# Seven block products for eight in the projections of the last two attention units, and a written order of issue

## Chip, cores and metric

The kernel runs on one core of one Trainium2 chip. The metric is the time of one execution on the device in microseconds (us); the time of a version is the median over its runs.

## The reference

A layer of two branches over the same input `x` (1 x 2048 x 640), mixed by a gate, all in float32.

```python
qkv = (x @ wqkv).reshape(B, S, 3, H, Dh)          # H = 32 heads of 20
idx = pos[:, None] - arange(8) * 2                 # eight keys, two apart
attn = softmax(where(idx >= 0, q . k[idx], -1e9) * scale)
a = (attn @ v[idx]).reshape(B, S, 640) @ wo
h = x @ w1 + b1                                    # 640 -> 1728
b = (h * tanh(softplus(h))) @ w2                   # Mish, 1728 -> 640
g = sigmoid((x * gate_w).sum(-1))
out = g * a + (1 - g) * b
```

## The kernel before

**Matrix work.** Each float32 operand is held as a rounded high part and the rest, a "pair" tile of 2 x 512 columns; one 128-deep product is three matmuls (`mm3`, lines 932 to 934: high by high, high by rest, rest by high). ACT makes the high part (line 873), DVE or POOL subtracts it from the operand for the rest (line 876). Operands come by DMA into `raw`, `z` or `hb` tiles, or into the pair's second half itself.

**Attention.** The work is cut into eight units `u = 4 * P + hq`: `P` is a half of the sequence (two blocks `tb` of 512 rows), `hq` a quarter of the heads. `qkv(u, half)` projects 512 rows in four PSUM banks: each bank is 128 rows by 496 columns (160 of q, 320 of k and v, 16 left-over columns of `w1`) over five blocks `kc` of 128, so 15 matmuls in a run. ACT empties a bank in three pieces (lines 1080 to 1084). DVE then does the unit's attention in sixteen instructions of 2560 columns (lines 985, 988, 1023, 1032) and small ones between them.

**First dense layer.** `quad(q, P, R)` (listed as T) makes two blocks of hidden columns for two row blocks by seven products of blocks for eight: sums of `x` blocks (`XS`, made once in each half by `sums_of_x`), sums of weight blocks, copies of one bank into another on ACT (line 1374) so that matmuls go on from a partial sum, and one addition of a kept product on DVE (line 1407). The projections of all eight units are plain before the change.

**Then** the second dense layer (`mlp2`, 7 products, `sums_of_w2` for its weights, listed as S), and the output projection. `FRONT` lists the first part's pieces in order, `BACK` says at which step of `mlp2` further pieces are put in.

**What sets the order.** All instructions are recorded as tasks, and `Plan.run` issues them. Before, it steps through a model of the five engines and takes, whenever an engine is free, the most urgent task that is ready; five tables of numbers by task (`MOVED`, `HELD_BACK`, `NEEDED`, `RANKED`, `ENGINE`) shift each task's place, delay, urgency, rank or engine. Tasks of kind "ANY" (rests, sums) go to DVE or POOL. On the chip each engine runs its list in this order and waits on semaphores; SP issues nearly all DMAs, POOL those that add in memory.

## Time and profile before

| | |
|---|---|
| median of 3 runs | 617.6 us (616.7 to 618.37) |
| profiled execution, its own time | 616.73 us |
| span in its profile | 615.0 us |
| PE busy | 608.9 us, 2693 matmuls |
| DVE, ACT, POOL busy | 577.1, 387.9, 311.2 us |

Busy times are unions of an engine's instructions. Matmuls overlap in the pipeline, so their rate is read from the distance of their starts.

### The profile page before, as it was taken

How to read it: one execution, taken by the hardware profiler on the slowest of the kernel's cores; microseconds unless marked ns; L12 is line 12 of the kernel's file. 1: busy time of each engine (PE TensorE's matmuls, PEld its weight loads, DVE VectorE, ACT ScalarE, POOL GpSimd, SP SyncE). 2: the span in 40 equal slices, each digit the busy share in tenths (PEclk: the TensorE clock that was granted, in tenths of full speed). 3: DMA queues.
4: the chain of work that ended last, by engine and by line, in shares of the span. 5: the costliest groups of instructions: out<-in, count | busy, mean ns of one | idle time of the engine just before them, and what ended most of it. 6: DMA issues, size and time to landing. Idle time of an engine off the chain costs nothing.

```text
span 615.0 us, 8940 instructions
## 1 busy us (share of the span) xinstructions
PE 608.9 (99%) x2693; PEld 504.7 (82%) x2693; DVE 577.1 (94%) x531; ACT 387.9 (63%) x854; POOL 311.2 (51%) x293
## 2 busy tenths in 40 slices
PE   8999999999999999999999999999999999999997
PEld 6888888888888888788888888888888888888885
DVE  4999999999998999999999999999999999999962
ACT  5746774768575767876666654583867574684721
POOL 2736566476283654654457657668554444601200
PEclk9999999999999999999999999999999999999999
DMA  8864679999999689999998999789999998996423
GB/s 301 254 192 149 178 220 305 280 252 305 257 268 300 172 240 273 261 242 259 291 267 219 286 289 290 243 245 299 332 377 352 283 386 276 321 354 197 147 89 119
DMA packets 106128, 159.43 MB, mean 259 GB/s; under 512 B 12112, under 2 KB 47952, under 8 KB 106048
## 3 DMA queue, kind: packets, MB, share of 16 engines
q1 hardware_dynamic: 98976, 146.01, 73.2%
q0 software_dynamic: 7104, 12.85, 13.7%
q8 instruction: 21, 0.34, 0.2%
q14 instruction: 27, 0.22, 0.1%
HBM read 91.90 MB, written 64.36 MB: 254 GB/s over the span
## 4 chain that ended last, share of the span: by engine, by line
PE 98%; DMA 1%; ACT 0%; SPq 0%; issue 0%; ACTq 0%
PE bank L932 32%; PE bank L934 32%; PE bank L933 32%; DMA z<-in_wq 1%; PE bank L1687 1%; PE bank L1688 1%; PE bank L1074 0%; SPq L882 0%; ACT pair L873 0%; ACT kvq L1801 0%; ACT kvq L1080 0%; ACT kvq L1082 0%; ACT hx L1084 0%; ACT zt L1086 0%; ACTq L1801 0%
## 5 line engine op out<-in xcount | busy, mean ns | idle before, releaser
L932 PE MATMUL bank<-pair,pair 128*128 128x512 f32 (+2 forms) x774 | 299.5, 387 | 0.4 <-ACT zt L1086 0.4
L933 PE MATMUL bank<-pair,pair 128*128 128x512 f32 (+2 forms) x774 | 299.7, 387 | 0.0
L934 PE MATMUL bank<-pair,pair 128*128 128x512 f32 (+2 forms) x774 | 299.7, 387 | 0.0
L932 PEld LDWEIGHTS bank<-pair,pair 128*128 128x128 f32 x774 | 145.4, 188 | 29.4 <-ACT zt L1086 0.8
L934 PEld LDWEIGHTS bank<-pair,pair 128*128 128x128 f32 x774 | 145.4, 188 | 28.7
L933 PEld LDWEIGHTS bank<-pair,pair 128*128 128x128 f32 x774 | 145.3, 188 | 28.7
L876 POOL TENSOR_TENSOR pair<-raw,pair 128x512 fp32r<-128x512 f32 (+3 forms) x82 | 104.8, 1303 | 86.9 <-ACT pair L873 30.2
L876 POOL TENSOR_TENSOR pair<-pair 128x512 fp32r<-128x512 f32 (+1 forms) x65 | 82.9, 1294 | 56.5 <-ACT pair L873 21.6
L873 ACT ACTIVATE pair<-pair 128x512 fp32r<-128x512 f32 (+1 forms) x139 | 79.6, 612 | 38.8 <-DMA pair<-act 18.7
L1023 DVE TENSOR_TENSOR pr<-kvq,side 128x2560 f32<-128x2560 f32 x32 | 90.3, 2822 | 1.1
L1032 DVE TENSOR_REDUCE kvq<-pr 128x320 f32<-128x2560 f32 x32 | 90.1, 2816 | 0.6
L988 DVE TENSOR_REDUCE lg<-pr 128x128 f32<-128x2560 f32 x32 | 90.0, 2812 | 0.6
L985 DVE TENSOR_TENSOR pr<-kvq,side 128x2560 f32<-128x2560 f32 x32 | 89.8, 2806 | 0.6 <-ACT lg L1000 0.5
L873 ACT ACTIVATE pair<-raw 128x512 fp32r<-128x512 f32 (+3 forms) x125 | 72.6, 613 | 18.5 <-PE bank L934 5.2
L1080 ACT ACTIVATE kvq<-bank 128x320 f32<-128x320 f32 x64 | 27.7, 434 | 49.1 <-PE bank L934 48.9
L876 DVE TENSOR_TENSOR pair<-pair 128x512 fp32r<-128x512 f32 (+1 forms) x74 | 46.7, 671 | 0.9 <-ACT pair L873 0.9
L932 PE MATMUL bank<-kvq,pair 128*128 128x512 f32 x102 | 40.0, 392 | 0.0
L933 PE MATMUL bank<-kvq,pair 128*128 128x512 f32 x102 | 39.8, 390 | 0.0
L934 PE MATMUL bank<-kvq,pair 128*128 128x512 f32 x102 | 39.8, 390 | 0.0
L1227 POOL TENSOR_TENSOR raw<-raw,raw 128x256 f32<-128x256 f32 (+1 forms) x25 | 24.4, 978 | 22.6 <-DVE side L1026 7.8
L876 DVE TENSOR_TENSOR pair<-raw,pair 128x512 fp32r<-128x512 f32 (+3 forms) x43 | 32.9, 785 | 1.7 <-ACT pair L873 1.7
L1374 ACT ACTIVATE bank<-bank 128x512 f32<-128x512 f32 x36 | 21.0, 584 | 13.7 <-PE bank L934 13.5
(119 smaller groups left out, 590.9 us busy)
## 6 DMA issues: line engine op xcount, KB each, us to landing
pair<-actt SPq DMA_DIRECT2D x54, 256.0 KB, 5.0
pair<-act SPq DMA_DIRECT2D x38, 256.0 KB, 4.8
raw<-in_w SPq DMA_DIRECT2D x34, 256.0 KB, 4.7
raw<-in_wq SPq DMA_DIRECT2D x30, 248.0 KB, 4.5
raw<-in_x SPq DMA_DIRECT2D x29, 256.0 KB, 5.1
actt<-hb SPq DMA_DIRECT2D x28, 256.0 KB, 3.6
actt<-z SPq DMA_DIRECT2D x24, 256.0 KB, 6.6
act<-z SPq DMA_DIRECT2D x24, 256.0 KB, 5.7
```

Of the source, the lines that this page charges most:

```text
L873: a = add("ACT", act_ns(n), lambda: A.activation(hi(), raw(), AF.Copy), after, rank=rank, take=take, hold=hold, kind="hi")
L876: return (V if e == "DVE" else G).tensor_tensor(lo(), raw(), hi().bitcast(F32), op=OP.subtract)
L932: nc.tensor.matmul(ps, ah, bh, start=first, stop=False, skip_group_check=more)
L933: nc.tensor.matmul(ps, ah, bl, start=False, stop=False, skip_group_check=more)
L934: nc.tensor.matmul(ps, al, bh, start=False, stop=last, skip_group_check=more)
L985: return V.tensor_tensor(pr, window(kv, s0, 0), qs[:, :, None, :].to_broadcast([128, 2, W, QF]), op=OP.mult)
L988: return V.tensor_reduce(lg_w[:, s0:s0 + 2], pr.rearrange("p s w (h d) -> p s w h d", d=DH), op=OP.add, axis=AX.X)
L1023: return V.tensor_tensor(twos, vw, pw[:, :, :, :, None, None].to_broadcast([128, 2, W, HQ, DH // 2, 2]), op=OP.mult)
L1032: return step("DVE", 2820, lambda: V.tensor_reduce(q[:, s0:s0 + 2].rearrange("p s (f j) -> p f s j", j=2), by_place, op=OP.add, axis=AX.X) ...
L1080: a = add("ACT", 330, lambda: A.activation(kv[:, 7 + s], ps.t[:, QF:3 * QF].rearrange("p (a b) -> p a b", a=2), AF.Copy), [done] + before, ...
L1227: return (V if e == "DVE" else G).tensor_tensor(t.t[:, i:i + n], a.t[:, j:j + n], b.t[:, k:k + n], op=op)
L1374: return add("ACT", 590, lambda: A.activation(to.t, of.t, AF.Copy), after, rank=-0.6, take=[to], hold=[of], kind=kind)
```

## The change

Units 6 and 7 (the second half of the sequence, head quarters 2 and 3) are no longer projected by `qkv` but together by a new function `qkv_two` (listed as D). The 2 x 2 blocks are rows `tb` 2 and 3 by even and odd `kc` of `x` (the sums `XS` are those of the quads), and even and odd `kc` by head quarter of the weights; the fifth `kc` is added plainly. `sums_of_wq(kp)` (U) makes four sums of weight blocks, stores them to memory, and `qkv_two` loads them again. What followed the projections in `qkv` (the halo copies, the attention) is now in `placed_unit`. S4 and S1, the sums of `w2` for two of its seven blocks, move from FRONT into BACK.

`Plan.run` no longer chooses: `ISSUE` lists each engine's tasks by number, `TAKEN` says on which engine the buffer of each ring is taken next, and the run places buffers only. The five tables are gone. A POOL task of kind "ANY" is made to follow the DVE instruction beside which the list puts it.

```diff
 FRONT = """q1 s0 Q00 Q01 w0 r00 Q10 q2 F0 F1 r10 Q11 r20 T00 r40 T10 Q20 S0 T20 r30 Q21 q3 T30 T40 Q30 w1
-r50 y3 q4 T50 Q31 x2 s1 F2 r01 Q40 F3 M0 T01 r11 r21 q5 r31 r51 S3 M1 T11 Q41 T21 Q50 r41 T31
-q6 Q51 T41 S2 q7 Q60 T51 H Q61 Q70 Q71 S4 S1"""
-BACK = "23O0 13V0 0M2 7S6 21O1 2S5 35G 0M3 21V1"
+r50 y3 q4 T50 Q31 x2 s1 F2 r01 Q40 F3 M0 T01 r11 r21 q5 r31 r51 S3 M1 T11 Q41 T21 Q50 U0 r41 T31
+U1 Q51 T41 S2 T51 D"""
+BACK = "23O0 13V0 1S4 0M2 7S6 3S1 21O1 5S5 35G 0M3 21V1"
...
+ENGINES = ("PE", "ACT", "DVE", "POOL", "SP")
+ISSUE = {
+    "PE": """1 96-110 115 120 125 130 135 140 145 290 232 240 236 244 298 294 267 263 302 376 377 380 381 386 388 425 389 390 426 429 430
...
+TAKEN = {
+    "bank": ("0000000000000000000000010101101100101010000000011100111000100101000000000010011010101000010101001010010000010110011"
...
+            if t.eng == "POOL" and t.both:
+                if single:
+                    s = max(s, over["DVE"] - 80)
+                elif before and s < over["DVE"]:
+                    s = max(s, before.own + 100)
+                if ahead and ahead[0] < s + t.ns - 50 and ahead[1].alone:
+                    s = max(s, ahead[0] + ahead[1].ns)
+            if t.eng == "DVE" and t.alone:
+                s = max(s, beside - 50)
...
+            if e == "POOL" and t.both:
+                gate = before if s < over["DVE"] - 80 else last
+                if gate and gate.ins and ins:
+                    self.follow(ins, gate.ins)
...
+    def sums_of_wq(kp):
+        r = {}
+        for hq, kc in ((2, 2 * kp), (3, 2 * kp), (3, 2 * kp + 1), (2, 2 * kp + 1)):
+            r[hq, kc - 2 * kp] = raw = raw_buf()
+            raw.ready = dma(lambda raw=raw: raw.t[:, :NCOL], lambda hq=hq, kc=kc: wq[hq, kc][:, :NCOL], rank=0.6, take=[raw], size=NCOL * 512)
+        b11, b21, b12, b22 = r[2, 0], r[2, 1], r[3, 0], r[3, 1]
+        t1 = sum_into((b11, 0), (b12, 0), (b11, 0), OP.subtract, [b11.ready, b12.ready], NCOL, rank=AHEAD)
+        t3 = sum_into((b12, 0), (b22, 0), (b12, 0), OP.subtract, [t1, b22.ready], NCOL, rank=AHEAD)
+        t2 = sum_into((b22, 0), (b22, 0), (b11, 0), OP.subtract, [t3], NCOL, rank=AHEAD)
+        t4 = sum_into((b21, 0), (b21, 0), (b22, 0), OP.subtract, [t2, b21.ready], NCOL, rank=AHEAD)
+        for i, raw, t in ((1, b11, t1), (3, b12, t3), (2, b22, t2), (4, b21, t4)):
+            wq_sum[kp, i] = [dma(lambda kp=kp, i=i: wq_d[kp, i], lambda raw=raw: raw.t[:, :NCOL], [t], rank=0.7, hold=[raw], size=NCOL * 512)]
+    def qkv_two():
+        n, t0, t1 = NCOL, 2, 3
+        def plain(hq, kc):
+            return load_pair(lambda: wq[hq, kc][:, :n], "ANY", n=n)
+        def summed(i):
+            return [load_pair(lambda kp=kp: wq_d[kp, i], "ANY", n=n, after=wq_sum[kp, i], inner=True) for kp in range(2)]
+        def xs(tb, b):
+            return [X[tb, 2 * kp + b] for kp in range(2)]
+        def s(i):
+            return [XS[kp, i] for kp in range(2)]
+        def phase(banks, xt, wt, after, start, stop, sums=False):
+            ends = []
+            for i, ps in enumerate(banks):
+                def run(i=i, ps=ps):
+                    for k, (a, b) in enumerate(zip(xt, wt)):
+                        mm3(ps.t[:, :n], tuple(a.t[:, j, i * 128:(i + 1) * 128] for j in range(2)), tuple(b.t[:, j, :n] for j in range(2)),
+                            start and k == 0, stop and k == len(xt) - 1, not start)
+                t = pe_add(3 * len(xt) * mm_ns(n), run, after[i] + sum((x.ready for x in xt + wt), []), take=[ps] if start else [], hold=[ps] + xt + wt)
+                ends.append([t])
+                if sums:
+                    s_uses.append(t)
+            return ends
+        def copy(to, of, after, take):
+            return add("ACT", 590, lambda: A.activation(to.t[:, :n], of.t[:, :n], AF.Copy), after, rank=-0.6, take=[to] if take else [], hold=[to, of])
+        def copies(tos, ofs, after, take):
+            return [[copy(to, of, t, take)] for to, of, t in zip(tos, ofs, after)]
+        def plus_five(to, five, after):
+            return add("DVE", 690, lambda: V.tensor_tensor(to.t[:, :n], five.t[:, :n], to.t[:, :n], op=OP.add), after, rank=SOON, hold=[to, five])
+        def both(*lists):
+            return [sum(x, []) for x in zip(*lists)]
+        def out_of(u, banks, half, ends):
+            ev = unit.setdefault(u, {})
+            for i, (ps, t) in enumerate(zip(banks, ends)):
+                ev[4 * half + i] = qkv_evac(u, 1, u - 4, 4 * half + i, ps, t[0])
+        none = [[] for _ in range(4)]
+        one = [ps_buf(n) for _ in range(4)]
+        b11 = [plain(2, 2 * kp) for kp in range(2)]
+        p1 = phase(one, xs(t0, 0), b11, none, True, True)
+        two_ = [ps_buf(0) for _ in range(4)]
+        c1 = copies(two_, one, p1, True)
+        b21 = [plain(2, 2 * kp + 1) for kp in range(2)] + [plain(2, 4)]
+        p2 = phase(one, xs(t0, 1) + [X[t0, 4]], b21, c1, False, True)
+        out_of(6, one, 0, p2)
+        p6 = phase(two_, s(2), summed(2), c1, False, False, True)
+        z = [z_buf() for _ in range(4)]
+        c3 = copies(z, two_, p6, True)
+        p7 = phase(two_, s(3), summed(3), c3, False, False, True)
+        w = [raw_buf(), h_buf(), raw_buf(), h_buf()]
+        c4 = copies(w, two_, p7, True)
+        p4 = phase(two_, xs(t1, 1) + [X[t1, 4]], summed(4) + [b21[2]], c4, False, True)
+        out_of(6, two_, 1, p4)
+        five = [ps_buf(n) for _ in range(4)]
+        p5 = phase(five, s(1), summed(1), none, True, True, True)
+        listed["H"]()
+        z5 = [[plus_five(a, b, t + c)] for a, b, t, c in zip(z, five, p5, c3)]
+        w5 = [[plus_five(a, b, t + c)] for a, b, t, c in zip(w, five, p5, c4)]
+        b22 = [plain(3, 2 * kp + 1) for kp in range(2)] + [plain(3, 4)]
+        three = [ps_buf(0) for _ in range(4)]
+        c5 = copies(three, z, z5, True)
+        p3 = phase(three, s(4) + [X[t0, 4]], b22, c5, False, True)
+        placed_unit(6)
+        out_of(7, three, 0, p3)
+        four = [ps_buf(0) for _ in range(4)]
+        c6 = copies(four, w, w5, True)
+        p8 = phase(four, [X[t1, 4]], [b22[2]], c6, False, True)
+        out_of(7, four, 1, p8)
+        placed_unit(7)
```

`phase` runs three matmuls for each operand pair in each of four banks; `copies` are ACT copies of one bank (or kept tile) to another; `plus_five` is a DVE addition of the fifth product to a kept one.

**First place: PE, in the projections of unit 6.** A name is a tile with its number; of a matmul's operands the weights' pair stands first, the rows' pair second. Before, `bank0_63` gets the last of its 15 matmuls over five blocks, three matmuls of a quad (512 columns) follow, and then the next bank is begun.

```order
L932 MATMUL bank0_63<-pair17_3114,pair0_1802 128x496
L933 MATMUL bank0_63<-pair17_3114,pair0_1802 128x496
L934 MATMUL bank0_63<-pair17_3114,pair0_1802 128x496
L932 MATMUL bank2_65<-pair0_1802,pair6_2843 128x512
L933 MATMUL bank2_65<-pair0_1802,pair6_2843 128x512
L934 MATMUL bank2_65<-pair0_1802,pair6_2843 128x512
L932 MATMUL bank6_69<-pair18_3025,pair10_2031 128x496 [waits DVE_49]
```

After the change (lines 511 to 513 are `mm3`) a bank gets two blocks in its first piece, and another bank, which was begun earlier and has been copied since, goes on.

```order
L511 MATMUL bank0_63<-pair12_3153,pair19_1801 128x496
L512 MATMUL bank0_63<-pair12_3153,pair19_1801 128x496
L513 MATMUL bank0_63<-pair12_3153,pair19_1801 128x496
L511 MATMUL bank6_69<-pair9_3081,pair2_1854 128x496 [waits Activation_49]
L512 MATMUL bank6_69<-pair9_3081,pair2_1854 128x496
L513 MATMUL bank6_69<-pair9_3081,pair2_1854 128x496
L511 MATMUL bank6_69<-pair1_3229,pair3_1936 128x496
L512 MATMUL bank6_69<-pair1_3229,pair3_1936 128x496 [waits Pool_49]
```

The run of 15 is cut into pieces: the second piece of `bank6_69` now waits for ACT, and at its second weight block for POOL, which makes that block's rest.

**Second place: DVE, in the attention of units 4 and 5, while units 6 and 7 are projected.** `pr` and `lg` are products and logits, `sm` the softmax's sums. Before, one rest of a weight block (`pair1_3298`) stands ahead of the softmax's small instructions.

```order
L988 TENSOR_REDUCE lg_223<-pr_225 128x2x8x8 [waits DVE_49]
L876 TENSOR_TENSOR pair1_3298<-raw7_3076,pair1_3298 128x496 [waits Activation_49]
L1015 TENSOR_REDUCE sm_227<-lg_223 128x32 [waits Activation_49]
L1016 RECIPROCAL sm_227<-sm_227 128x32 [waits DVE_49]
L1017 TENSOR_TENSOR sm_227<-sm_227,gate_80 128x32 [waits DVE_49]
L1026 TENSOR_TENSOR side_224<-lg_223,sm_227 128x2x8x8 [waits DVE_49,Activation_49]
L1023 TENSOR_TENSOR pr_225<-kvq1_221,side_224 128x16x80x2 [waits DVE_49]
```

After the change four of the eight `plus_five` (line 776, a PSUM bank added to a kept tile) stand in such a place.

```order
L564 TENSOR_TENSOR pr_225<-kvq1_221,side_224 128x2560 [waits DMAHW3_49]
L567 TENSOR_REDUCE lg_223<-pr_225 128x2x8x8 [waits DVE_49]
L776 TENSOR_TENSOR z2_3419<-bank4_67,z2_3419 128x496 [waits DMAHW0_49,DMAHW7_49,PE_49,Activation_49]
L776 TENSOR_TENSOR z0_3394<-bank2_65,z0_3394 128x496 [waits PE_49,DMAHW4_49,Activation_49,Pool_49]
L776 TENSOR_TENSOR raw1_3457<-bank2_65,raw1_3457 128x496 [waits DMAHW5_49,Activation_49]
L594 TENSOR_REDUCE sm_227<-lg_223 128x32 [waits Activation_49]
L595 RECIPROCAL sm_227<-sm_227 128x32 [waits DVE_49]
L776 TENSOR_TENSOR hb1_3454<-bank4_67,hb1_3454 128x496 [waits DMAHW3_49,DMAHW0_49,DMAHW5_49,DMASW5_49,DMAHW6_49,DMASW1_49,DMASW0_49]
L596 TENSOR_TENSOR sm_227<-sm_227,gate_80 128x32 [waits DVE_49]
L605 TENSOR_TENSOR side_224<-lg_223,sm_227 128x2x8x8 [waits DVE_49]
```

The rest has left DVE here, and additions have come that name PE among their waits, with the softmax's sums and the next product `pr` queued behind them.

**Third place: POOL, while unit 6 is projected.** Lines 876 and 455 make rests; a row with `raw` inside reads a plain operand, one with the pair alone an operand that landed in the pair. Before, the plain weight blocks of units 6 and 7 stand here, and sums of the one quad whose results are added on chip (line 1328).

```order
L876 TENSOR_TENSOR pair2_3038<-raw7_2868,pair2_3038 128x496 [waits DVE_49,DMAHW6_49,PE_49,Activation_49]
L1170 DMA actt2_1_3_151<-actt1_1_3_137 128x512 [waits DMAHW7_49,DMASW5_49,DMASW0_49]
L876 TENSOR_TENSOR pair4_3072<-raw8_2910,pair4_3072 128x496 [waits DVE_49,DMAHW6_49,PE_49,Activation_49]
L876 TENSOR_TENSOR pair7_3084<-raw0_2914,pair7_3084 128x496 [waits Activation_49]
L876 TENSOR_TENSOR pair3_3151<-raw1_3056,pair3_3151 128x496 [waits DVE_49,DMAHW7_49,Activation_49,Pool_49]
L1328 TENSOR_TENSOR hb0_3086<-hb0_3086,hb1_3130 128x512 [waits DMAHW6_49,DMAHW5_49,Activation_49]
L1328 TENSOR_TENSOR hb1_3130<-hb1_3130,z1_3052 128x512 [waits DVE_49,Activation_49,Pool_49]
```

After the change the summed weight blocks come back from memory into pairs, and their rests stand on POOL.

```order
L455 TENSOR_TENSOR pair18_3113<-pair18_3113 128x496 [waits DMAHW2_49,DVE_49]
L455 TENSOR_TENSOR pair22_3204<-pair22_3204 128x496 [waits DMAHW5_49,DVE_49,Activation_49]
L455 TENSOR_TENSOR pair15_3095<-pair15_3095 128x496 [waits DMAHW7_49,DVE_49,Activation_49]
L455 TENSOR_TENSOR pair6_3148<-pair6_3148 128x496 [waits DMAHW1_49,DVE_49]
L1128 TENSOR_TENSOR raw7_3199<-raw7_3199 128x128 [waits DMAHW4_49]
L851 DMA actt3_0_6_161<-pair11_2984 64x512 [waits DMASW1_49]
L1009 TENSOR_TENSOR z3_3140<-z3_3140,z0_3134 128x512 [waits DMAHW3_49,DMASW3_49,DVE_49]
L455 TENSOR_TENSOR pair17_3247<-pair17_3247 128x496 [waits DMAHW4_49,PE_49]
```

Five of the eight rests of summed blocks stand in these eight rows; all eight are on POOL, and so are seven of the eight weight sums themselves.

## Rows read from the trace of the kernel before

**Rows 1.** The page: busy time of each engine

```profile
PE 608.9 (99%) x2693; PEld 504.7 (82%) x2693; DVE 577.1 (94%) x531; ACT 387.9 (63%) x854; POOL 311.2 (51%) x293
```

**Rows 2.** The page: the chain that ended last, by engine

```profile
PE 98%; DMA 1%; ACT 0%; SPq 0%; issue 0%; ACTq 0%
```

**Rows 3.** Waits of PE: us in total, times, longest

```profile
PE bank L856 <- DVE lg L852: 1.2, 1, 1.2
PE bank L932 <- ACT zt L1086: 0.4, 1, 0.4
PE bank L1074 <- ACT pair L873: 0.4, 1, 0.4
```

**Rows 4.** Timeline of PE at its longest stop: start, us, line

```profile
250.65 0.38 PE L934 MATMUL bank<-pair,pair 128*128 128x498 f32 x1
251.46 0.50 PE L932 MATMUL bank<-pair,pair 128*128 128x512 f32 x1 [0.42 <-ACT zt L1086]
```

**Rows 5.** Timeline of PE at the start

```profile
4.70 2.98 PE L1074 MATMUL bank<-pair,pair 128*128 128x498 f32 x12
8.06 2.98 PE L1074 MATMUL bank<-pair,pair 128*128 128x498 f32 x12 [0.37 <-ACT pair L873]
```

**Rows 6.** One long window: busy PE, PEld, DVE, ACT, POOL, clock, DMA share, GB/s

```profile
20.00:560.00 540.00, 539.58 (x2400) 450.15 (x2399) 528.68 (x457) 357.16 (x799) 298.68 (x280) 1.00 0.92 270
```

**Rows 7.** Timeline of PE in a projection of unit 6 or 7

```profile
349.63 0.38 PE L933 MATMUL bank<-pair,pair 128*128 128x496 f32 x1
349.85 0.38 PE L934 MATMUL bank<-pair,pair 128*128 128x496 f32 x1
...
351.39 0.38 PE L932 MATMUL bank<-pair,pair 128*128 128x496 f32 x1
```

**Rows 8.** Groups by form: count, busy us, mean ns, idle before

```profile
L932 PE MATMUL bank<-pair,pair 128*128 128x496 f32 x240 | 91.8, 383 | 0.0
L876 POOL TENSOR_TENSOR pair<-pair 128x512 fp32r<-128x512 f32 x59 | 76.9, 1322 | 41.0 <-ACT pair L873 18.5 <-DVE side L1026 6.9 <-PE bank L934 5.8
L876 DVE TENSOR_TENSOR pair<-pair 128x512 fp32r<-128x512 f32 x65 | 42.7, 692 | 0.9 <-ACT pair L873 0.9
L876 DVE TENSOR_TENSOR pair<-raw,pair 128x512 fp32r<-128x512 f32 x30 | 23.0, 783 | 0.6 <-ACT pair L873 0.6
L1374 ACT ACTIVATE bank<-bank 128x512 f32<-128x512 f32 x36 | 21.0, 584 | 13.7 <-PE bank L934 13.5
L873 ACT ACTIVATE pair<-raw 128x496 fp32r<-128x496 f32 x30 | 17.8, 621 | 3.6 <-issue 2.2 <-POOL pair L876 0.9 <-PE bank L934 0.5
L1010 ACT ACT_TABLE_LOAD x13 | 16.7, 1283 | 0.2
L1407 DVE TENSOR_TENSOR z<-bank,z 128x512 f32<-128x512 f32 x22 | 15.0, 681 | 2.9 <-PE bank L934 2.9
L876 DVE TENSOR_TENSOR kvq<-raw,kvq 128x512 fp32r<-128x512 f32 x14 | 12.1, 878 | 0.0
```

**Rows 9.** DMA: queue's packets, MB, share; a weight block's KB, us to landing

```profile
q1 hardware_dynamic: 98976, 146.01, 73.2%
raw<-in_wq SPq DMA_DIRECT2D x30, 248.0 KB, 4.5
```

**Rows 10.** Windows of 20 us around the projections of units 6 and 7

```profile
300.00:320.00 20.00, 20.00 (x91) 16.75 (x90) 19.78 (x17) 15.09 (x33) 11.18 (x10) 1.00 1.01 267
320.00:340.00 20.00, 20.00 (x91) 16.77 (x90) 19.69 (x14) 11.23 (x29) 14.82 (x18) 1.00 0.89 235
340.00:360.00 20.00, 20.00 (x93) 17.04 (x92) 19.66 (x16) 12.11 (x30) 13.44 (x15) 1.00 1.02 296
360.00:380.00 20.00, 20.00 (x93) 17.06 (x91) 19.72 (x15) 11.21 (x35) 12.19 (x12) 1.00 1.04 277
```

**Rows 11.** Line 876 on DVE: duration in ns, least/median/most

```profile
L876 DVE TENSOR_TENSOR pair<-raw,pair x43: 282/682/1787, 5.3 to 591.5; 128x512 fp32r<-128x512 f32 x30, 128x496 fp32r<-128x496 f32 x9, 128x498 fp32r<-128x498 f32 x3, 128x128 fp32r<-128x128 f32 x1
L876 DVE TENSOR_TENSOR kvq<-raw,kvq x14: 672/680/1787, 22.7 to 584.2; 128x512 fp32r<-128x512 f32 x14
```

More of the change, by code (lines that the diff above doesn't have):

```diff
@@ L47, with __init__ @@
 class Buf:
-    def __init__(self, ring, make):
-        self.ring, self.make, self.left, self.t, self.gone, self.can = ring, make, 0, None, None, None
+    def __init__(self, ring, make, n=None, seeded=False):
+        self.ring, self.make, self.n, self.seeded, self.left, self.t, self.ended = ring, make, n, seeded, 0, None, 0.0
 class Ring:
     def __init__(self, n):
-        self.free, self.line, self.at, self.left = n, [], 0, list(range(n))
+        self.free, self.at = [(0.0, i) for i in range(n)], 0
 class Late:
@@ L565, in run @@
     def run(self):
-        ready = {e: [] for e in self.LAG}
-        busy = dict.fromkeys(self.LAG, False)
-        events, n, left, wire = [], 0, len(self.tasks), 0.0
-        quiet, gate, last, shared, begun = 0.0, None, None, [], False
-        LARGE, TOUCH = ("qk", "qk sum", "pv"), ("qk", "w", "pv")
-        inside = {"DVE": "", "ACT": ""}
-        touched = copied = None
-        moved, held, needed, ranked, engine = map(table, (MOVED, HELD_BACK, NEEDED, RANKED, ENGINE))
-        for i, t in enumerate(self.tasks):
-            t.key = (t.rank, i + moved.get(i, 0))
-            t.late += held.get(i, 0)
-            t.bias, t.only, t.turn = needed.get(i, 0), engine.get(i, 0), t.rank + ranked.get(i, 0)
-            t.rdy = 0.0
-            if not t.waits:
-                (shared if t.both else ready[t.eng]).append(t)
@@ L601, in fits @@
-        def fits(t):
+        TOUCH = ("qk", "w", "pv")
+        lines = {}
+        for e, text in ISSUE.items():
+            line = lines[e] = []
+            for x in text.split():
+                a, _, b = x.partition("-")
+                line.extend(self.tasks[i] for i in range(int(a), int(b or a) + 1))
+            for t in line:
+                assert t.eng == e or t.both and e in ("DVE", "POOL")
+                t.eng = e
+                if type(t.ns) is tuple:
+                    t.ns = t.ns[e == "DVE"]
@@ new lines, in run, with places @@
+        assert len({id(t) for line in lines.values() for t in line}) == len(self.tasks) == sum(map(len, lines.values()))
+        at, left, free, wire = dict.fromkeys(lines, 0), len(self.tasks), dict.fromkeys(lines, 0.0), 0.0
+        over, kind = dict.fromkeys(lines, 0.0), dict.fromkeys(lines, "")
+        beside, single, before, last, touched, copied, whole = 0.0, False, None, None, None, None, set()
+        taken = {self.rings[k]: v for k, v in TAKEN.items()}
+        def places(b):
+            return [x for x in b.ring.free if not b.seeded or x[1] in whole]
@@ L602, in fits, with start @@
+        def start(t):
+            s = free[t.eng]
+            for p in t.after:
+                if p.done is None:
+                    return None
+                s = max(s, p.own if p.eng == t.eng and not p.land else p.done)
             want = {}
             for b in t.take:
-                want[b.ring] = want.get(b.ring, 0) + 1
-                if b.ring.free < want[b.ring] or b.ring.line[b.ring.at + want[b.ring] - 1] is not b:
-                    return False
-                if b.can and not b.can():
-                    return False
@@ L720 @@
+        return max(t.done for t in self.tasks)
 @with_exitstack
@@ L743, in ps_buf @@
     def ps_buf(n=512, seeded=False):
[L745 to L757 removed]
+        b = plan.buf("bank", lambda: banks[b.slot], n, seeded)
         return b
@@ L876, in low @@
             return (V if e == "DVE" else G).tensor_tensor(lo(), raw(), hi().bitcast(F32), op=OP.subtract)
-        b = add(eng, either(eng, n), low, [a], rank=rank, hold=list(take) + list(hold))
+        b = add(eng, either(eng, n), low, [a], rank=rank, hold=list(take) + list(hold), alone=True)
         return [a, b]
@@ L1550, in load_step @@
         loaded[i] = p, at, acts
[L1552 removed]
     def place():
[L1556 to L1563 removed]
+        b = plan.buf("b", lambda: kvq[1][:, b.slot * 512:(b.slot + 1) * 512])
         return b
```

329 lines of the change are left out of this document (131 added, 198 removed), and 497 rows, old and new, of tables (ENGINE, HELD_BACK, ISSUE, MOVED).

## The prediction

> **What bounds the kernel now.** Read the page's busy times first [rows 1]: PE has work in 608.9 of 615.0 us, DVE in 577.1, ACT and POOL far less. The chain that ended last says that this is no accident of one stage: 98% of it is PE [rows 2]. Then PE's waits by releaser [rows 3]: three stops, 2.0 us in all, one of them before the first input has landed. The reader is to see who is missing there: no operand made by POOL, and no DMA, is ever named. The longest stop inside the run is one at 250.65 us, where the next start follows after 0.81 us in place of 0.23 [rows 4], so 0.58 us are lost; at the start 0.37 us pass before the second weight block's high part is there [rows 5]. From 20 to 560 us PE is busy in 539.58 of 540 us, DVE in 528.7, ACT in 357.2, POOL in 298.7 [rows 6]. So PE paces the program by its count of matmuls, and DVE, with 11.3 us to spare, is close behind.
>
> PE's busy time is no price list, since matmuls overlap: the 496-column ones last 383 ns by their rows [rows 8], but eight starts in a row lie 349.63 to 351.39 us apart, 0.220 us each [rows 7]. A matmul that goes is worth 0.220 us.
>
> **The change, part by part.** *PE.* For each of the four places of a 128-row piece, units 6 and 7 took 2 row blocks x 2 units x 5 blocks = 20 operand pairs of three matmuls. Now the phases take 2+3+2+2+3+2+3+1 = 18. That is 4 x 3 x 18 = 216 matmuls for 240, all of one form, none moved off PE: 24 x 0.220 = **5.3 us** less on the path that sets the end.
>
> *ACT.* The 20 copies of a partial sum cost what bank copies cost in the quads, 584 ns, so 11.7 us; 16 weight operands in place of 10 add six high parts of 621 ns, 3.7 us; and counted over the order there are 24 table loads for 30, each 1283 ns, 7.7 us less [rows 8]. The net 7.7 us lie beside PE: ACT is idle for 183 of the 540 us [rows 6]. What could show is a copy's latency, as a bank can't go on before it. The cover is the other banks: while one is copied, three others have six matmuls each, 18 x 0.220 = 4.0 us against 0.58 us. With no cover at all, 20 copies would cost 11.7 us.
>
> *DVE and POOL.* The eight additions of the fifth product are DVE's, 8 x 0.681 = 5.4 us. Counted over the whole order DVE has 16 other instructions fewer: 8 rests of landed operands, 4 of row sums in `kvq`, 3 of raw operands, 1 small one: 8 x 0.692 + 4 x 0.878 + 3 x 0.783 = 11.4 us [rows 8]. DVE's load falls by 6 us. POOL has 30 two-input instructions more (229 become 259: the 16 new weight sums and rests, and what left DVE); at 1.322 us [rows 8], which is too much for the few narrow ones, that is 40 us, over idle time of 241 us [rows 6]. An operand whose rest goes from DVE to POOL is ready 0.63 us later (1.322 less 0.692), which costs nothing as long as operands are ready that much ahead, and PE's waits without a POOL in them [rows 3] say that so far they are. If this cover is gone, 15 of them cost up to 9.5 us. In the second place shown above, additions that wait for PE now stand on DVE ahead of the softmax's sums and of the next 2560-column product, so a late PE would hold attention. The quads' like additions waited 2.9 us in 22 cases [rows 8], so eight may wait 1.1 us, out of DVE's spare.
>
> *DMA.* Six plain weight blocks more to load, eight sums to store and eight to load again: 22 transfers of 0.254 MB, 5.6 MB. The hardware queue moved 146 MB in 73.2% of 615 us [rows 9], 324 GB/s, so this is 17.2 us of its time. It falls into a stretch where the DMA share is 0.89 to 1.04 already [rows 10]. Out of the same stretch go S4 and S1, each 0.66 MB in and 0.66 MB out, 8.1 us. Net, 9 us more traffic over some 100 us. A weight block lands 4.5 us after its issue [rows 9]; SP waits for a free tile ahead of a load, and whatever stands behind that load waits too. Price if hidden: nothing. If the whole excess comes in front of PE: 9 us.
>
> *The written order as such* removes and adds no work. It could gain the two stops named above, 0.6 + 0.4 = 1.0 us, and the loss has no bound in the rows of before, except that all waits of PE there come to 2.0 us.
>
> *Sum.* For stops I take the 0.8 us that PE waited inside the run [rows 3] as staying in the time of before, and as much again for four phases that hand banks from ACT to PE, a value near the rows since all those of before are this small: 616.73 - 5.28 + 0.8 = 612.25 us, against the profiled execution's own 616.73 (span 615.0 and 1.7 around it). The median of the three runs, 617.6, stands 0.9 above that execution; for a median I add half of it: **612.6 us**. The bounds: 616.73 - 5.28 - 1.0 = 610.4 with both old stops gone and no new one; and upward what the rivals give.
>
> **Rivals.** *Nothing is left of it: POOL's rests come late.* Place: the summed blocks in the third excerpt, and then the second dense layer, whose operands' rests have partly gone to POOL. Two rests that become ready together are 1.322 us apart, so four operand pairs that PE meets one POOL instruction early cost 5.3 us, all of the gain: 617 us, no change that can be told. For it: an order that is fixed can't pass a ready task ahead of a late one, and PE waits there by name for POOL in the first excerpt. Against: POOL is idle 45% of the long window, and PE never waited for it [rows 3, 6].
>
> *DMA takes the place of PE in the projections.* Place: the first matmuls on summed weights. A half of the 9 us gives 616.7, all of it 621 us. For: the DMA share [rows 10]. Against: the sums depend on the input alone, so they can be loaded, made and stored long before they are used.
>
> *Slower: POOL blocks DVE.* A rest on DVE takes 682 ns in the median, but up to 1787 [rows 11], 1.1 us more with the same form, and what differs between two such rests is what POOL does beside them. If each of the 30 new POOL instructions did this once, DVE would have 33 us more. In the changed kernel the long window is 534.7 us, DVE's work in it 528.7 - 6 = 522.7, the spare 12.0; the other 21 us would show: 612.6 + 21 = 634 us. It turns into a loss of over 0.3% (1.9 us) when 12.0 + 5.3 + 1.9 - 0.8 = 18.4 us are lost, so when 17 of 30 block. Against it: the means are only 0.10 us above the median for the raw rests and 0.20 for those in `kvq` [rows 8, 11], 43 x 0.10 + 14 x 0.20 = 7 us over the 229 POOL instructions there are, 0.03 each, and 30 more would add 0.9 us.
> The Trainium skill, page "SBUF — State Buffer", section "SBUF: two separate sides", states the mechanism: a DVE instruction with two SBUF inputs and a GpSimd one that reads SBUF lock the same port pair, whichever starts first keeps it to its end, and the other blocks. By that rule every POOL instruction that is begun ahead of a DVE rest costs that rest up to its own length. The trace agrees that it happens (1787 ns) and shows that it is rare (783 ns in the mean).
>
> **How the numbers follow.** The forecast has 0.72, and reaches from 610.4 to 615.5 (three more us of stops). POOL late: 0.14, 614.5 to 618.5. DMA: 0.07, 615 to 621. DVE blocked: 0.07, from 619 up. About 0.3%, 1.9 us, is what a measurement of this kernel can tell from no change: below 615.7 is faster. Faster gets nearly all of the forecast and half of the POOL case, 0.78; same the rest of that and some of DMA, 0.13; slower 0.09. A range of 610.4 to 617.0 leaves out the upper third of the POOL case, half of DMA and all of DVE blocked, less than 0.2.
>
> **What will show it.** Right: 24 matmuls fewer, all with 496 columns; PE's span shorter by 5 us with its waits still below 3 us; the chain 98% PE; DVE's busy time 4 to 8 us and ACT's no more than 10 us away from before; POOL's near 350 us. Wrong: POOL rests or DMA landings among PE's waits by more than 2 us (the first two rivals); DVE's rests with means well above 0.8 us and its busy share at 97% or more (the third). The forecast fails if the stops of PE come to 4 us or more, wherever they are.

## The result, and the profile after

| | before | after |
|---|---|---|
| median, lowest to highest of 20 runs each | 618.49 us (616.28 to 622.87) | 621.15 us (618.14 to 626.7) |
| profiled execution | 616.73 us | 623.77 us |
| stops of PE, worked out | 3.1 us | 15.7 us |

The ratio is 1.0045 (95%: 1.0023 to 1.0066): the changed kernel is slower by 0.45%, where 0.8% faster was forecast, and its median lies above the whole range. The stops in the last row are the distances between starts of PE beyond the pitch (0.220 to 0.227 us), added up over a profiled execution; matmuls at the lower clock, told of below, are in it. Between the two profiled executions they grow by 12.6 us, the 24 matmuls give back 5.3, which leaves 7.3; their times differ by 7.0. So the stops account for the loss. These two executions stand further apart than the medians, which differ by 2.7 us: the one after is longer than most of its 20 (its granted clock over the run is 0.994, as in two others), so by the medians the stops grew by some 8 us (an estimate, 2.7 + 5.3). The question is where the stops come from.

The page of the changed kernel, which answers to [rows 1] and [rows 9]:

```profile
PE 610.0 (98%) x2669; PEld 502.9 (81%) x2669; DVE 563.4 (91%) x523; ACT 386.1 (62%) x874; POOL 343.1 (55%) x323
q1 hardware_dynamic: 102144, 151.60, 75.9%
```

There are 24 matmuls fewer. DVE's work fell by 13.7 us, ACT's by 1.8, POOL's grew by 31.9, and the queue carries 5.6 MB more, as reckoned. None of the busy times looks like a loss. The waits of PE by releaser, which answer to [rows 3]:

```profile
PE bank L511 <- ACT kvq L1258: 3.7, 1, 3.7
PE bank L511 <- ACT bank L1258: 1.2, 2, 1.0
...
PE bank L1360 <- POOL pair L1173: 0.8, 1, 0.8
PE bank L513 <- POOL pair L455: 0.7, 1, 0.7
```

The 1.2 us on `lg` of [rows 3], left out here, stay. These are new, and the longest is a wait for ACT, which has 38% of the span free. Windows tell when the time was lost. First the kernel after, then the kernel before (the count behind PE is what to read):

```profile
0.00:400.00 400.00, 398.57 (x1764) 331.63 (x1765) 373.56 (x306) 263.98 (x632) 235.59 (x228) 1.00 0.92 261
400.00:445.00 45.00, 39.26 (x155) 30.58 (x154) 37.31 (x32) 27.88 (x58) 29.68 (x30) 0.92 0.96 273
445.00:560.00 115.00, 113.67 (x498) 92.91 (x498) 109.97 (x121) 68.55 (x138) 62.53 (x55) 1.00 0.98 322
```

```profile
0.00:400.00 400.00, 398.00 (x1767) 331.12 (x1768) 382.46 (x298) 263.23 (x615) 228.18 (x224) 1.00 0.91 254
400.00:445.00 45.00, 45.00 (x200) 37.28 (x199) 43.43 (x41) 31.47 (x60) 29.56 (x26) 1.00 0.94 290
445.00:560.00 115.00, 115.00 (x508) 95.07 (x508) 113.96 (x137) 74.86 (x147) 47.28 (x39) 1.00 0.96 326
```

At 400 us the changed kernel has 2669 - 1764 = 905 matmuls to go, the kernel before 2693 - 1767 = 926. It is 21 ahead, 4.6 us: the seven products have paid. In the next 45 us, the start of the second dense layer, it does 45 matmuls fewer, 10.2 us at 0.227, and up to 560 us another 10, 2.3 us. Its PE timeline at the longest stop:

```profile
406.05 0.39 PE L513 MATMUL bank<-pair,pair 128*128 128x512 f32 x1
410.09 0.80 PE L511 MATMUL bank<-pair,pair 128*128 128x512 f32 x1 [3.66 <-ACT kvq L1258]
410.69 0.63 PE L512 MATMUL bank<-pair,pair 128*128 128x512 f32 x1
411.11 0.63 PE L513 MATMUL bank<-pair,pair 128*128 128x512 f32 x1
...
412.82 0.51 PE L511 MATMUL bank<-pair,pair 128*128 128x512 f32 x1
```

PE stands for 4.05 us, and then five starts stand 0.42 to 0.43 us apart in place of 0.23, twice the distance. The window above has a granted clock of 0.92 where the others have 1.00: these matmuls ran at the lower level, 1.2 GHz, so this stop cost more than its length. Five more such distances follow from 441.45 us, after stops of 1.4, 0.6 and 1.2 us. ACT's timeline tells what the named copies were doing:

```profile
398.15 1.15 ACT L452 ACTIVATE pair<-pair 128x512 fp32r<-128x512 f32 x2 [3.17 <-DMA pair<-act]
402.10 0.45 ACT L579 ACTIVATE lg<-bound 1x24 f32<-1x24 f32 x3 [2.80 <-DVE lg L567]
402.57 1.28 ACT L863 ACT_TABLE_LOAD   x1
406.91 0.72 ACT L863 ACTIVATE pair<-pair,bias 64x512 f32<-64x512 f32 x1 [3.05 <-DMA pair<-h]
...
408.51 1.53 ACT L1258 ACTIVATE kvq<-bank 128x512 f32<-128x512 f32 x3
```

ACT waited 3.17 us for operands (`act`), 2.80 us for logits from DVE, and 3.05 us for reloaded hidden columns (`h`), and all of these stand in its list ahead of the copies PE needs. The first and the last are DMAs. So SP's timeline is the next one to read, after:

```profile
391.80 0.37 SPq L461 DMA_DIRECT2D s<-raw  x1
392.27 0.38 SPq L461 DMA_DIRECT2D pair<-act  x1
392.70 0.90 SPq L461 DMA_DIRECT2D s<-raw  x2
393.65 0.48 SPq L461 DMA_DIRECT2D raw<-in_w  x1
394.22 0.44 SPq L461 DMA_DIRECT2D pair<-act  x1
...
395.19 0.43 SPq L461 DMA_DIRECT2D s<-raw  x1
...
396.19 0.62 SPq L461 DMA_DIRECT2D pair<-act  x1
...
397.89 0.62 SPq L461 DMA_DIRECT2D pair<-h  x1
```

and before:

```profile
393.07 0.34 SPq L882 DMA_DIRECT2D s<-raw  x1
393.63 0.77 SPq L882 DMA_DIRECT2D h<-pair  x2
394.50 2.75 SPq L882 DMA_DIRECT2D pair<-act  x4
```

SP hands out one transfer in 0.3 to 0.7 us in these rows, with hardly a pause. Before, four operand blocks follow one another here; after, three operand blocks stand among sums being stored (`s<-raw`, S4 and S1) and their inputs (`raw<-in_w`). The last row after is the late `h` block. It landed at 406.89 us, 9.0 us after its issue, and ACT went on at 406.91. All eight transfers that SP issued from 396.19 to 401.74 us took 6.9 to 9.0 us, a halo copy of 560 KB just ahead of the `h` block among them; from 380 to 445 us in the kernel before none took more than 6.1. So at this stop it was the landing that was long, and not the wait for SP's turn alone; what made it long, no run shows. The DMA issues from 380 to 445 us, first before, then after:

```profile
DMA packets 13695, 18.16 MB, mean 279 GB/s; under 512 B 1647, under 2 KB 6916, under 8 KB 13690
...
pair<-act SPq DMA_DIRECT2D x16, 256.0 KB, 4.0
...
s<-raw SPq DMA_DIRECT2D x5, 128.0 KB, 2.8
...
s<-raw SPq DMA_DIRECT2D x3, 64.0 KB
```

```profile
DMA packets 14306, 17.56 MB, mean 270 GB/s; under 512 B 1631, under 2 KB 9260, under 8 KB 14300
...
pair<-act SPq DMA_DIRECT2D x11, 256.0 KB, 4.3
s<-raw SPq DMA_DIRECT2D x14, 128.0 KB, 4.4
...
s<-raw SPq DMA_DIRECT2D x8, 64.0 KB, 2.8
```

Over this longer stretch the bytes are no more, SP's issues are as many (100 before, 101 after), and in the median a block of `act` lands 4.3 us after its issue for 4.0. What differs is which transfers have these turns. Worked out from the timelines, an operand of a matmul was ready in the median 14.8 us ahead of its first use between 380 and 400 us, and 8.1 us between 400 and 445; in the changed kernel 5.3 and 2.1 us, some not at all.

### The profile page after: what moved, and what is told of

Read it like the earlier page. It is cut to its first block, busy times and chain, and to the rows that moved or that the text cites. A ratio compares the mean times of both kernels' runs of the same rounds, so it can differ in the third digit from the quotient of the medians.

```text
span 622.0 us, 8936 instructions
## 1 busy us (share of the span) xinstructions
PE 610.0 (98%) x2669; PEld 502.9 (81%) x2669; DVE 563.4 (91%) x523; ACT 386.1 (62%) x874; POOL 343.1 (55%) x323
## 5 line engine op out<-in xcount | busy, mean ns | idle before, releaser
L511 PE MATMUL bank<-pair,pair 128*128 128x512 f32 (+2 forms) x742 | 289.4, 390 | 4.9 <-ACT kvq L1258 3.7
L512 PE MATMUL bank<-pair,pair 128*128 128x512 f32 (+2 forms) x742 | 289.2, 390 | 0.6 <-POOL pair L455 0.4
L513 PE MATMUL bank<-pair,pair 128*128 128x512 f32 (+2 forms) x742 | 288.7, 389 | 0.7 <-POOL pair L455 0.7
L511 PEld LDWEIGHTS bank<-pair,pair 128*128 128x128 f32 x742 | 140.1, 189 | 34.2 <-ACT kvq L1258 4.1
L512 PEld LDWEIGHTS bank<-pair,pair 128*128 128x128 f32 x742 | 140.2, 189 | 29.7 <-POOL pair L455 1.3
L513 PEld LDWEIGHTS bank<-pair,pair 128*128 128x128 f32 x742 | 140.0, 189 | 28.7 <-POOL pair L455 1.0
L455 POOL TENSOR_TENSOR pair<-raw,pair 128x512 fp32r<-128x512 f32 (+4 forms) x82 | 104.8, 1302 | 82.0 <-ACT pair L452 41.3
L455 POOL TENSOR_TENSOR pair<-pair 128x512 fp32r<-128x512 f32 (+2 forms) x83 | 105.6, 1292 | 63.8 <-ACT pair L452 27.4
L452 ACT ACTIVATE pair<-pair 128x512 fp32r<-128x512 f32 (+2 forms) x147 | 83.9, 611 | 47.0 <-DMA pair<-actt 17.0
L452 ACT ACTIVATE pair<-raw 128x512 fp32r<-128x512 f32 (+4 forms) x123 | 74.0, 621 | 33.5 <-DVE raw L908 12.1
L908 POOL TENSOR_TENSOR raw<-raw,raw 128x256 f32<-128x256 f32 (+2 forms) x33 | 33.2, 1007 | 46.5 <-DVE pair L455 17.2
L455 DVE TENSOR_TENSOR pair<-pair 128x512 fp32r<-128x512 f32 (+2 forms) x64 | 42.3, 693 | 5.4 <-ACT pair L452 5.4
L455 DVE TENSOR_TENSOR pair<-raw,pair 128x512 fp32r<-128x512 f32 (+3 forms) x41 | 27.6, 691 | 9.4 <-ACT pair L452 9.4
```

Of the source, the lines that this page charges most:

```text
L452: a = add("ACT", act_ns(n), lambda: A.activation(hi(), raw(), AF.Copy), after, rank=rank, take=take, hold=hold, kind="hi")
L455: return (V if e == "DVE" else G).tensor_tensor(lo(), raw(), hi().bitcast(F32), op=OP.subtract)
L511: nc.tensor.matmul(ps, ah, bh, start=first, stop=False, skip_group_check=more)
L512: nc.tensor.matmul(ps, ah, bl, start=False, stop=False, skip_group_check=more)
L513: nc.tensor.matmul(ps, al, bh, start=False, stop=last, skip_group_check=more)
L908: return (V if e == "DVE" else G).tensor_tensor(t.t[:, i:i + n], a.t[:, j:j + n], b.t[:, k:k + n], op=op)
```

## The experiments

Theory: the moved sums S4 and S1 take the operands' turns in the second dense layer (place), by the number of their transfers and not by their bytes (means), and the written order has no lead left to bear it. Rivals: bytes; POOL's additions for the sums; one badly placed run of copies on ACT; POOL blocking DVE; the written order whatever the sums do. Each median stands with its ratio to the kernel before on the same chip (617.0 to 617.9 us there). What a run wins or loses is worked out from the ratios, of 617.6 us, the changed kernel's being 1.0045.

**Where and how much.** In `e1_no_s41` the changed kernel's S4 and S1 are left out, instructions and transfers, the rest stands in its order:

```diff
+    s_d[1] = s_d[4] = s_d[0]
+        begun = len(plan.tasks)
+        if kc in (1, 4):
+            for t in plan.tasks[begun:]:
+                t.fn = lambda *a: None
```

> The changed kernel, in which the sums S4 and S1 of w2 (18 transfers, 10 additions on POOL, 2 copies on ACT) are left out and sums of an earlier piece are loaded in their place, so that the second dense layer has wrong numbers for two of its seven blocks. Theory 'traffic' (the sums that were moved into the second dense layer stand on the DMA queue ahead of its operands): the stops of PE between 400 and 445 us and the lower clock behind them, 10 us, go for the most part, 612 to 615 us. Theory 'order' (an instruction that could run stands behind one that waits, whatever the queue carries): at most 2 us less, 619 to 621 us. Theory 'products' (the 216 matmuls with their copies and stored sums cost what they save): no change, 621 us.

616.33 us, 0.997 (0.9949 to 0.999): 4.6 us less than the changed kernel, but still 3.1 above the forecast. The window that lost 45 matmuls gets nearly all back. It stands first, then a row of PE's waits in this run:

```profile
400.00:445.00 45.00, 44.66 (x197) 36.38 (x196) 43.72 (x36) 31.47 (x64) 35.49 (x36) 1.00 0.99 305
```

```profile
PE bank L512 <- ACT bank L1056: 1.0, 3, 0.6
```

The 7.0 us of stops that stay are small and strewn over the run, copies of the first dense layer's quads among them. ACT's timeline at one:

```profile
229.21 0.63 ACT L453 ACTIVATE pair<-raw 128x512 fp32r<-128x512 f32 x1 [5.40 <-DMA raw<-t]
229.74 0.58 ACT L1056 ACTIVATE bank<-bank 128x512 f32<-128x512 f32 x1
```

The copy could have gone earlier. It stands behind a high part whose operand lands late, and a written list doesn't pass it.

**One place on ACT.** `e2_act_first` puts the four copies of 408 us ahead of the hidden columns in ACT's list:

```diff
+PUT = [('ACT', 1887, 1746), ('ACT', 1889, 1746), ('ACT', 1883, 1746), ('ACT', 1885, 1948)]
+        for e, x, y in PUT:
+            lines[e].remove(self.tasks[x])
+            lines[e].insert(lines[e].index(self.tasks[y]), self.tasks[x])
```

> The changed kernel with four copies of product a's banks put ahead of the Mish of the reloaded hidden columns in ACT's list, nothing else. Theory 'order': the stop of 4.05 us at 406 us goes and with it the lower clock behind it (1.5 us), 615 to 617 us. Theory 'traffic': the operands are late all the same, so PE meets the next late one; the stop shrinks by 1 to 2 us and the others grow, 619 to 621 us.

620.58 us, 1.0056 (1.0028 to 1.0084), no gain. The stop of 4.05 us shrinks to 1.15, and others of 2.3, 1.3 and 1.6 us follow at 412, 418 and 431 us, now for rests (PE waits 2.8 us for POOL's and 1.7 us for DVE's). ACT's order was what showed; the operands were late behind it.

**Traffic put into the kernel before.** `e3_before_traffic` adds 21 transfers of 128 KB from memory to memory to the old kernel, one behind every third of SP's from 405 us on; `e6_before_issues` the same transfers of 1 KB:

```diff
+                    if e == "SP" and now > 405000 and len(self.extra) < 21:
+                        self.seen += 1
+                        if self.seen % 3 == 0:
+                            self.extra.append(self.more(len(self.extra)))
-    plan.more = lambda i: nc.sync.dma_start(spare[i], w2[i % KH][:, :256])
+    plan.more = lambda i: nc.sync.dma_start(spare[i][:1], w2[i % KH][:1, :256])
```

> The kernel before with 21 more transfers of 0.131 MB from memory to memory (2.75 MB, about what S4 and S1 and the sums pushed back behind them add to the changed kernel between 380 and 445 us), one behind every third transfer that SP issues in that stretch. Theory 'traffic': 8 us of the hardware queue, of which the operands' lead of 6 to 15 us in the kernel before hides a part; 620 to 626 us, with PE waiting for ACT's high parts. Theories 'order' and 'products': the old order lets what is ready pass, 618 to 619 us.

> The kernel before with 21 more transfers at the places of the earlier run, but of 1 KB each (one row of 256 elements) instead of 128 KB. If bytes cost the 6.7 us there, this is 617 to 618.5 us, as before. If the issue slots on SP cost it (21 x 0.4 us, everything behind them issued later), it is 622 to 625 us.

624.49 us, 1.0108 (1.0071 to 1.0145), and 623.18 us, 1.0091 (1.0066 to 1.0116). A transfer of 1 KB costs nearly what one of 128 KB does; the intervals overlap. In `e6_before_issues` the added transfers (least, median and most ns, first and last start), PE's longest wait, and the windows in which it is lost:

```profile
L2045 SPq DMA_DIRECT2D spare<-in_w x21: 494/495/599, 407.3 to 460.8; - x21
```

```profile
PE bank L939 <- DVE pair L882: 4.3, 2, 3.9
```

```profile
420.00:440.00 20.00, 18.86 (x82) 14.96 (x81) 19.15 (x12) 9.58 (x20) 14.13 (x14) 1.00 0.89 252
440.00:460.00 20.00, 15.46 (x60) 12.35 (x61) 15.03 (x21) 12.53 (x25) 6.84 (x6) 0.91 0.95 298
```

The added bytes are 21 KB in all, the DMA engines have 11 and 5% free in these windows, and 21 x 0.495 = 10.4 us of SP's turns are spent. So bytes aren't needed for such a loss. It also shows that the old order, with its longer lead, breaks too when it gets transfers that it was not made for.

**The parts of S4 and S1.** `e5_no_s41_sums` keeps all their transfers and leaves out their eight wide additions on POOL; `e10_small_stores` cuts their twelve stores to one row each:

```diff
+                if kc in (1, 4) and n == 256:
+                    return None
```

```diff
+            if kc in (1, 4):
+                return dma(lambda: row_d[kc][:1, c:c + n], lambda: b.t[:1, i:i + n], after, rank=0.5, hold=[b], size=n * 512)
```

> The changed kernel with all 18 transfers of S4 and S1, but without eight of their ten additions on POOL (5.9 us of POOL's work), so that blocks stored for two of the seven w2 pieces are not summed. If the bytes on the queue are what holds the second dense layer up ('traffic'), nothing is won: 620 to 621.5 us, stops of 8 us or more between 400 and 445 us. If it is POOL's work in that stretch that makes the rests late, the gain of the run without S4 and S1 comes back: 616 to 617 us.

> The changed kernel with the 12 stores of S4 and S1 cut to one row each (1.3 MB less, the same number of issues), and sums of an earlier piece loaded in place of theirs, so that two of seven w2 pieces are wrong. Issue slots: no change, 620 to 621.5 us. Bytes on the queue: half of what leaving out S4 and S1 gave, 618 to 619 us.

619.87 us, 1.0033 (1.0006 to 1.006), and 620.19 us, 1.0047 (1.0029 to 1.0065). POOL's additions are worth 0.7 us, within the intervals, and the stores' bytes nothing. `e9_fewer_stores` joins two pairs of the six stores of each sum of `w2`, 14 issues fewer with the same bytes, and `e14_before_fewer` does this to the kernel before:

```diff
+        k[1].fn = lambda: nc.sync.dma_start(s_d[kc][:, 256:768], a1.t)
+        k[5].fn = lambda: nc.sync.dma_start(s_d[kc][:, 512:].rearrange("p (a c) -> p a c", a=2)[:, :, 256:],
+                                            apart.t[:, 256:].rearrange("p (a c) -> p a c", a=2))
+        k[2].fn = k[4].fn = lambda: None
```

> The changed kernel with two pairs of the six stores of each sum of w2 joined, so that the same bytes go out in four transfers (14 issues fewer on SP over the whole kernel, 8 of them between 360 and 445 us). If issue slots on SP hold up the second dense layer, 8 x 0.4 us of them come back: 617 to 619 us. If bytes do, 621 us.

> The kernel before with the same joined stores as in the run that won 2.5 us on the changed kernel. If the joined stores gain only because the changed order has nothing to spare on SP, the kernel before, whose operands are ready 6 to 15 us early in that stretch, gains nothing: 616.5 to 618 us. If fewer transfers are a gain of their own, 614.5 to 616 us.

618.56 us, 1.0021 (1.0007 to 1.0036), 1.5 us less than the changed kernel, and 616.66 us, 1.0006 (0.9982 to 1.003). Fewer transfers seem to help where operands arrive just in time (the interval overlaps that of the changed kernel), and show no gain in the kernel before.

**SP's turn, or the transfer?** `e13_stores_on_act` has ACT issue the twelve stores, `e15_issues_on_act` the 1 KB transfers in the kernel before (`A.dma_start` for `nc.sync.dma_start`):

> The changed kernel with the 12 stores of S4 and S1 issued by ACT (where they stand 1.5 us after the time that they had in SP's list) in place of SP; bytes, number of transfers and everything else as they are. If what is short is SP's turn, 12 x 0.45 us of it come free between 380 and 445 us and a good part of what leaving out S4 and S1 gave comes back: 617 to 619.5 us. If every transfer costs the same whoever issues it, 620 to 621.5 us, or more where ACT's high parts now stand behind a store.

> The kernel before with the same 21 transfers of 1 KB at the same places, issued by ACT in place of SP; they wait for nothing, so nothing stands behind a wait. If SP's turn is what costs (0.5 us each, for everything behind it), the kernel is free of it: 617 to 618.5 us. If a transfer costs the operands' loads whoever issues it, 621 to 624 us, as from SP.

The first took 626.17 us, 1.0143 (1.0124 to 1.0162), and tells nothing on the question: ACT's timeline shows a row of stores that waits for POOL's sums with all high parts behind it.

```profile
388.79 6.25 ACTq L1142 DMA_DIRECT2D s<-raw  x4
395.13 0.53 ACT L1156 ACTIVATE pair<-raw 128x384 fp32r<-128x384 f32 x1 [6.15 <-POOL pair L463]
```

The second took 621.13 us, 1.0058 (1.0037 to 1.0079), 3.6 us over the kernel before for 5.6 from SP, with intervals that overlap. The cost doesn't vanish with SP's turns. The trace shows a reason: the transfers of SP and ACT share eight semaphores in turn, and an issue waits until the last transfer that had its semaphore has landed. Nothing reads the tiles of the added transfers, and yet SP waits for their landing, from 380 to 445 us:

```profile
SPq L888 <- DMA spare<-in_w: 2.4, 5, 0.8
```

Worked out from the traces, SP's waits for the semaphore of its next transfer come to 9.6 us in this stretch in the kernel before, 8.4 with the transfers on SP, and 16.3 with them on ACT. So a transfer has two prices here: 0.5 us of its engine's turn, and one of eight places until it lands, 3.6 us in the median of those from ACT. ACT's own turns lie on the operands' way too, so the two stay apart only in part.

**POOL and DVE.** `e4_no_gate` lets POOL's two-input instructions go without following DVE's (`self.follow(ins, gate.ins)` becomes `pass`):

> The changed kernel without the dependence of a POOL rest or sum on the DVE instruction beside it; data alone decides. If these gates hold POOL's rests back (a part of 'order'), the operands are ready up to 1 us earlier and 1 to 3 us are won, 618 to 620 us. If POOL blocks DVE when it runs freely, the rests on DVE get longer (means over 0.75 us) and the time rises to 623 us or more. With 'traffic' alone: no change.

657.4 us, 1.064 (1.0598 to 1.0682). One group of DVE's rests by line, after, and in this run:

```profile
L455 DVE TENSOR_TENSOR pair<-pair 128x512 fp32r<-128x512 f32 (+2 forms) x64 | 42.3, 693 | 5.4 <-ACT pair L452 5.4
```

```profile
L455 DVE TENSOR_TENSOR pair<-pair 128x512 fp32r<-128x512 f32 (+2 forms) x64 | 52.1, 849 | 0.0
```

The same 523 instructions take DVE 620.4 us for 563.4; the softmax's subtraction (line 588) takes 1596 ns in the mean for 532. Ungated, this is by far the largest cost in the case; in the changed kernel the gates hold it off.

**The order.** `e7_raw_11` gives the changed kernel two more `raw` tiles (11 for 9); `e8_other_order` and `e11_new_order` keep its tasks and PE's list and put the lists of the other engines in other orders. These lists also choose anew whether DVE or POOL makes a rest or a sum: in `e11_new_order` 54 of 426 change engine. In `e8_other_order` the attention's instructions don't keep their sequence, so a part of its result is made of other data.

> The changed kernel with 11 raw tiles in place of 9 (they fit), the lists as they are. If a part of the operands' lateness comes from SP, which stands at a load until a raw tile is free, loads are issued earlier and 1 to 4 us are won, 617 to 620 us. If SP doesn't wait for tiles in the stretch from 380 to 460 us (its waits there name PE and landings, 4.7 us and less), 621 us.

> The same tasks as in the changed kernel, PE's list untouched, but ACT's, DVE's, POOL's and SP's lists in another order, one made so that operands are ready some 2 us earlier and copies of banks don't stand behind high parts whose operands have not landed; a few rests change between DVE and POOL. Theory 'order': the operations of the change are all there, S4 and S1 too, and the 5.3 us come out: 609 to 614 us, PE's waits below 4 us. Theory 'traffic' in its strict form (too many bytes for the queue between 380 and 445 us in any order): 617 us or more. Theory 'products': 617 us or more.

> The same tasks, tiles and PE list as in the changed kernel; ACT's, DVE's, POOL's and SP's lists in an order made for operands that land up to 1.5 us later than the given order seems to need, the attention's instructions left in their sequence. If the loss lies in the order of the four lists, the stops of PE fall to 4 us or less and the 5.3 us of the 24 matmuls come out: 610 to 614 us. If the stretch is short of issue slots or bytes in any order: 616 to 620 us.

620.8 us, 1.0046 (1.0014 to 1.0077); 620.11 us, 1.0022 (0.9993 to 1.005); 617.04 us, 0.9988 (0.9965 to 1.001). Tiles alone bring nothing. Other lists alone bring 3.5 us with the same instructions and transfers (order and choice of engine stay together here): operands are then ready 10.6 us ahead between 380 and 400 us and 3.2 up to 445. The longest stop is now a wait for POOL:

```profile
421.14 0.39 PE L519 MATMUL bank<-pair,pair 128*128 128x512 f32 x1
423.65 0.50 PE L520 MATMUL bank<-pair,pair 128*128 128x512 f32 x1 [2.12 <-POOL pair L463]
```

**All of it together.** `e12_order_and_room` has the 11 tiles, the joined stores and an order made for both; `e16_spare_order` another such order, made with later landings.

> The same with 11 raw tiles, an order made for them, and the joined stores of the other run. Order: 610 to 613 us. If slots and tiles are what is short, this one gains and the order alone does not: 612 to 615 us against 616 to 620.

> The changed kernel's work with joined stores, 11 raw tiles and an order of the four lists made for landings later still than the order of the run before (PE's list as it is). By 'order': PE's stops near 3 us in all and 612 to 615 us. If the order of the run before was at its end, the same 615 us.

615.38 us, 0.9966 (0.9953 to 0.998), and 615.17 us, 0.9951 (0.993 to 0.9973): both beat the kernel before, by 2.1 and 3.0 us, and the changed one. Of the 5.3 us of the matmuls, 2.3 are still missing in the better of them. In `e12_order_and_room` PE stops for 4.1 us in all and the stretch that lost 10.2 us is full, with S4 and S1 in it:

```profile
400.00:445.00 45.00, 45.00 (x200) 36.93 (x198) 44.02 (x41) 31.42 (x63) 31.72 (x31) 1.00 0.98 288
```

The profiled execution of `e16_spare_order` has full windows there too, but 8.0 us of stops elsewhere; which of the two orders is better, the runs don't tell.

The median lead doesn't tell a full window from one with stops. Between 400 and 445 us it is 2.2 us in `e1_no_s41`, 2.6 in `e12_order_and_room` and 1.6 in `e16_spare_order`, all nearly full or full, and 2.1 in the changed kernel, which lost 45 matmuls there. Just ahead, between 380 and 400 us, it is 7.3, 9.3 and 7.2 us in these three for 5.3.

## Why the prediction was wrong

- **24 x 0.220 = 5.3 us: right.** 4.6 us are there at 400 us, and with the stops back near their old sum the profiled execution of `e12_order_and_room` took 613.79 us, 2.9 less than that of before.
- **ACT's, POOL's and DVE's loads: right or better.** POOL took 343 us (forecast near 350). ACT was to rise by 7.7 us and fell by 1.8, inside the 10 us allowed. DVE fell by 13.7 us for 6: its raw rests take 691 ns for 785, those in `kvq` 687 for 878, sums in `raw` 642 for 733; 41, 11 and 31 of them make 8.8 us. Without the gates (`e4_no_gate`) the same three take 752, 919 and 917 ns, so it is the blocking of [rows 11] that has gone. The third rival's mechanism is real, but here it ran the other way.
- **DMA in the projections: right.** No stop names them, and PE is ahead when they end.
- **The step that failed** is "*The written order as such* removes and adds no work", costed at 0 to -1.0, and with it the 0.8 us of stops in the sum. Measured, the stops grew by 12.6 us in the profiled execution (some 8 by the medians), and other lists for the same tasks bring 3.5 us back (`e11_new_order`). The sentence "the loss has no bound in the rows of before" was written and then left out of the range; the waits of PE before, 2.0 us, were taken as a guide to those after, though they belonged to the order that was being removed.
- **The second failure** is in the DMA term. "Out of the same stretch go S4 and S1" counted 8.1 us as relief where the sums left, and priced nothing where they went. There they cost 4.6 us (`e1_no_s41`). The bytes of the stores are no part of it (`e10_small_stores`) and POOL's additions little (`e5_no_s41_sums`); that transfers cost without bytes is shown on the kernel before (`e6_before_issues`), and for S4 and S1 themselves it is likely but not shown apart, as `e9_fewer_stores` stays within the noise. A price in MB would have failed as well. 3.1 us against the forecast remain without them; small stops are what the trace of that run still shows.
- **The first rival** had the right second place, and a price near what S4 and S1 cost, but another releaser: POOL is named in 1.9 us of PE's waits, just under the 2 us written down as the sign. Behind ACT's order it does show, with 2.8 us in `e2_act_first` and 3.2 in `e11_new_order`. Its argument, that a fixed order can't pass a ready task ahead of a late one, holds for ACT and SP too, and that is what happened.
- The test written down held: stops over 4 us, wherever they are, and the forecast fails.

Open: how much of a transfer's cost is the issuing engine's turn and how much its place among eight; what made the landings at the longest stop last 6.9 to 9.0 us; how much of the order's loss is sequence and how much the choice between DVE and POOL; and where the last 2.3 us are. Settled is that the order and the moved sums cost most of the gain, and not the seven products, which are in `e12_order_and_room` and `e16_spare_order` too.

## What to carry to other kernels

Price a moved step where it goes, transfer by transfer, on the queue that hands them out. When the order of issue is replaced, the old kernel's waits say nothing about the new one's: read how long before its use each operand is ready, and look at the operands that come last. A short lead is a warning and no price. A saving of work can be kept by an order made for it; look at the order before giving up the work.
